# Attention and expert router: a later reciprocal of the gates, and a reordered set-up

## The chip, the cores and the metric

The kernel runs on one core of a Trainium2 chip. The metric is device time in microseconds (us) of one execution, from launch to end. The time before is the median of three runs; the profile is that of one more execution, with its own time. Engines are called as in the profile: PE (TensorE; PEld is its weight load), DVE (VectorE), ACT (ScalarE), POOL (GpSimd) and SP (SyncE, which here only issues DMAs).

## The reference

Two stages in one launch. First block-sparse attention: 4 sequences of 768 tokens, 8 heads of 64, 24 blocks of 32 tokens; a query block sees its neighbours, the first and the last block, and three random blocks whose numbers come in as int64.

```python
mask = np.abs(blk_i - blk_j) <= 1
mask = mask | (blk_i == 0) | (blk_j == 0) | (blk_i == n_blocks - 1) | (blk_j == n_blocks - 1)
for qb in range(n_blocks):
    for kb in sampled_blocks[qb]:
        mask[qb*block:(qb+1)*block, kb*block:(kb+1)*block] = True
scores = np.where(mask, scores, -1e9)
...
x = attn_out.transpose(0, 2, 1, 3).reshape(B * S, H * D)
```

Then a router over 8 experts for the 3072 rows x of 512: logits are the cosines of x with the expert embeddings over tau, the expert is the argmax, the gate its softmax probability, and the row's output is `gate * relu(x @ w1[e]) @ w2[e]`.

## The kernel before

**Attention** takes about the first half of the span. The 4 sequences have 4 pairs of heads each; a pair is 12 units (2 halves of the queries times 6 chunks of keys), so a sequence is 48 units, and `u % 48` is the unit that a plan speaks of. For each unit the program writes down `attend_fast(u)` and then `score_fast(u + 2)` (the loop in `attention_fast`, L835 to L861):

- `score_fast`: PE adds the mask (`sc<-qmask,kmask`, bf16) and the scores (`sc<-qt,kt`, f32) in PSUM; ACT takes the exponential `e` (L342).
- `attend_fast`: DVE adds the `e` of a half up in `esum` (L355 for the first two, L357 for the others), PE multiplies `e` with the values into `av` (L360). Behind the sixth unit ACT copies one half of `av` to `part` (L364), and DVE adds the other to it as `at` (L366). There is one `av` buffer: the next half's first `av` matmul on PE has to wait for `at`.
- `turn_fast`: every sixth unit PE transposes half of the next pair's keys and queries into the PSUM tile `turn` (L322); `kt` (L325) and `qt` (L326) are its copies in SBUF.
- `settle`, at the fourth unit of the next half: PE transposes `at` back (`back`, L388), sums `esum` (L395); DVE divides (L398 to L408) and writes the rows `x` and the partial logits `part`. `squares` then lets POOL square `x` and add it up in a tree (L419, L423). `turn`, `back`, `tp` (the turned embeddings) and `rk` (of `rank`) share one PSUM buffer, `small`.

**Routing** of a finished sequence is a generator, `route`, that is taken a step further at certain units of the next sequence; `after_sequence` holds the table of these units, written by hand. Its steps: sums on POOL (norm, partial logits); norm, logits and maximum on DVE; exponential on ACT and choice on DVE (`pick`, `oh`); counts `seen` (six additions, L514) and the gate's denominator on POOL (`ex_l`, `x` column 512; L516 to L519), one by one between the squares of the same unit; the reciprocal of the gates on DVE (L521); then the DMAs of the rows `x` to DRAM. `rank` multiplies `oh` and `seen` on PE (`rk`, L535 to L537). All steps are put down with `issue_after` behind the last `esum` and `e`, and a scheduler then merges them into each engine's in-order queue.

**Experts** follow: 27 tiles of 128 rows, whose weights (4 MB a tile) come by DMA into three buffers.

**Set-up** before unit 0: `load_first` loads the first pair in halves and the block numbers (`ids`), POOL makes the identity, `build_mask` makes `kmask` and `qmask` (DVE, POOL, a matmul `qr` on PE, and a copy of one half each by DVE and ACT, L148), `turn_fast(0, 0)` turns the first half. At u = 3 `build_experts` normalises the expert embeddings: squares on ACT (L194), power on POOL (L195), three DVE steps (L196 to L198), four transposes on PE (`tp`, L201), copies on DVE (`en`, `back`).

Of the kernel before, what the change touches and what calls it, by code (L numbers as in the profile page):

```python
# [11 lines left out]
F32 = mybir.dt.float32  # L12
I32 = mybir.dt.int32
# [34 lines left out]
def two_banks(k, name):  # L48
    return k.small.tile([P, 2, 512], F32, name=name, tag="small")
# [9 lines left out]
def build_ident(k):  # L59
    k.ident = k.const.tile([P, P], F32, name="ident")  # L60
    make_identity(k.nc, k.ident[:])
# [29 lines left out]


def load_ids(k):
    nc, pool = k.nc, k.setup
    k.ids = pool.tile([NB, NRAND], I32, name="ids")
    words = dataclasses.replace(k.blocks.tensor, shape=[NB, 2 * NRAND], dtype=I32)
    with nc.allow_non_contiguous_dma(reason="low words of the block numbers"):
        nc.sync.dma_start(out=k.ids, in_=bass.AP(tensor=words, offset=0, ap=[[2 * NRAND, NB], [2, NRAND]]))


def block_mask(k, exact=False):

    nc, pool = k.nc, k.setup
    dif = iota(k, "dif", [NB, NB], [[1, NB]], mult=-1)
    col = iota(k, "col", [NB, NB], [[1, NB]])
    row = iota(k, "row", [NB, NB], [[0, NB]], mult=1)
    m = pool.tile([NB, NB], F32, name="m")
    nc.vector.tensor_tensor(out=m, in0=dif, in1=dif, op=ALU.mult)
    nc.vector.tensor_scalar(out=m, in0=m, scalar1=1.5, scalar2=None, op0=ALU.is_le)
    for val in (0.0, float(NB - 1)):  # L110
        for pos in (col, row):
            ins = nc.vector.scalar_tensor_tensor(out=m, in0=pos, scalar=val, in1=m, op0=ALU.is_equal, op1=ALU.max)
    ids_f = pool.tile([NB, NRAND], F32, name="ids_f")
    with k.tc.issue_after(ins.ins):
        nc.vector.tensor_copy(out=ids_f, in_=k.ids)
    for r in range(NRAND):
        nc.vector.scalar_tensor_tensor(out=m, in0=col, scalar=ids_f[:, r:r + 1], in1=m,
                                       op0=ALU.is_equal, op1=ALU.max)
    both = pool.tile([NB, 2, D], F32 if exact else BF16, name="both")
    if not exact:  # L120
        nc.gpsimd.memset(both, 0.0)
    nc.vector.tensor_scalar(out=both[:, :, 0:NB], in0=m.unsqueeze(1).broadcast_to([NB, 2, NB]), scalar1=1.0,
                            scalar2=-NEG, op0=ALU.subtract, op1=ALU.mult)
    return both
# [62 lines left out]


def build_experts(k):
    nc, pool = k.nc, k.setup  # L190
    emb, tau = k.emb_rows, k.tau_rows
    sq = pool.tile([E, DM], F32, name="emb_sq")
    nrm = pool.tile([E, 1], F32, name="emb_nrm")
    nc.scalar.activation(sq, emb, ACT.Square, accum_out=nrm)  # L194
    nc.gpsimd.tensor_tensor(out=nrm, in0=nrm, in1=k.half[0:E, 0:1], op=ALU.pow)  # L195
    nc.vector.tensor_scalar(out=nrm, in0=nrm, scalar1=1e-6, scalar2=tau[:, 0:1], op0=ALU.add, op1=ALU.mult)  # L196
    nc.vector.reciprocal(out=nrm, in_=nrm)
    nc.vector.tensor_scalar(out=emb, in0=emb, scalar1=nrm[:, 0:1], scalar2=None, op0=ALU.mult)  # L198
    tp = two_banks(k, "tp")[:, 0]
    for c in range(ND):  # L200
        nc.tensor.transpose(tp[:, c * E:(c + 1) * E], emb[:, c * P:(c + 1) * P], k.ident[0:E, 0:E])  # L201
    k.en = k.const.tile([P, ND, E], F32, name="en")
    nc.vector.tensor_copy(out=k.en, in_=tp[:, 0:ND * E].rearrange("p (c e) -> p c e", e=E))
    k.back = k.const.tile([P, NPAIR, D + E], F32, name="back")
    for h in range(2):
        rows = slice(D * h, D * (h + 1))
        nc.vector.tensor_copy(out=k.back[rows, :, 0:D],
                              in_=k.ident[rows, rows].unsqueeze(1).broadcast_to([D, NPAIR, D]))
        nc.vector.tensor_copy(out=k.back[rows, :, D:D + E], in_=k.en[rows])


def load_pair(k, g, parts=(0, 1, 2), engine=None):
# [96 lines left out]
def turn_fast(k, g, part):  # L309

    nc = k.nc
    if part == 0:
        k.turned[g] = [k.tp.tile([P, NC, 2, D], F32, name=f"{n}t", tag=f"{n}t") for n in ("k", "q")]
    ps = two_banks(k, "turn")[:, :, 0:2 * NQ * D].rearrange("p r (n c t) -> p r n c t", n=2, t=D)
    chunks = slice(part * NQ, (part + 1) * NQ)
    for n in range(2):
        src = k.loaded[g][n][part] if g == 0 else k.loaded[g][n][:, :, chunks]
        for c in range(NQ):
            for r in range(2):
                toks = slice(D * r, D * (r + 1))  # L320
                for h in range(2):
                    nc.tensor.matmul(ps[D * h:D * (h + 1), r, n, c, :], lhsT=src[toks, h, c, :],  # L322
                                     rhs=k.ident[toks, toks], start=True, stop=True)
    kt, qt = [t[:, chunks].rearrange("p c r t -> p r c t") for t in k.turned[g]]
    nc.vector.tensor_copy(out=kt, in_=ps[:, :, 0])  # L325
    nc.scalar.mul(out=qt, in_=ps[:, :, 1], mul=SCALE)  # L326


# [142 lines left out]
def route(k, b):  # L471
# [47 lines left out]
    nc.gpsimd.tensor_scalar(out=gate, in0=gate, scalar1=1e-9, scalar2=None, op0=ALU.add)  # L519
    yield  # L520
    nc.vector.reciprocal(out=gate, in_=gate)  # L521
    drams = (k.x_early, k.x_dram) if b < EARLY else (k.x_dram,)
    for dram in drams:
        for c in range(NC):
# [266 lines left out]
def after_sequence(n, b):  # L791

    routing = partial(next, route(n, b), None)
    plan = [(7, routing), (10, routing), (11, routing), (12, routing), (14, partial(rank, n, b))]
    plan += [(13, routing)] + [(15 + NC * (i // 4), routing) for i in range(NC * (1 + (b < EARLY)))]
    if b == EARLY - 1:
        step = partial(next, dispatch_early(n), None)
        plan += [(u, step) for u in range(16, 39) if u % 3]
        plan += [(40, partial(fetch_rows, n, 0)), (41, partial(fetch_rows, n, 1))]
        step = partial(next, fetch_weights(n, 0, 4), None)  # L800
        plan += [(u, step) for u in (27, 27, 33, 33, 39, 39, 45, 45)]
    if b == EARLY:
        step = partial(next, fetch_weights(n, 1, 4), None)
        plan += [(u, step) for u in (3, 3, 9, 9, 27, 27, 33, 33)]
        plan += [(44, partial(prepare, n, 0))]
    return plan


def attention_fast(n, ctx):
    def pool(name, bufs, **kw):  # L810
        return ctx.enter_context(n.tc.tile_pool(name=name, bufs=bufs, **kw))

    n.acc, n.big = pool("acc", 1, space=PSUM), pool("big_f", 2, space=PSUM)
    n.ld, n.tp, n.ep = pool("ld", 3), pool("tp", 2), pool("ep", 4)
    pairs = B * NPAIR
    units, per = pairs * 2 * NC, 2 * NC
    n.masked = []
    setup = ExitStack()
    n.setup = setup.enter_context(n.tc.tile_pool(name="setup", bufs=1))
    load_first(n)  # L820
    build_ident(n)
    build_mask(n)
    turn_fast(n, 0, 0)
    score_fast(n, 0)
    score_fast(n, 1)
    turn_fast(n, 0, 1)
    with n.tc.issue_after(n.masked[0]), n.tc.issue_after(n.masked[1]):
        build_consts(n)
    load_pair(n, 1)
    load_experts(n)  # L830
    zero = n.const.tile([1, XW], F32, name="zero")
    n.nc.vector.memset(zero, 0.0)
    n.nc.sync.dma_start(n.x_dram[N:N + 1, :], zero)
    plan = []
    for u in range(units):  # L835
        g = u // per
        if u % per == 0 and g + 2 < pairs:
            load_pair(n, g + 2)
        if u % NC == 3 and NC < u < units - 2 * NC:
            settle(n, u // NC - 1)  # L840
        if u % NC == 4 and NC < u < units - 2 * NC:
            squares(n, u // NC - 1)
        if u == 3:
            with n.tc.issue_after(n.summed.ins), n.tc.issue_after(n.exps.ins):
                build_experts(n)
            setup.close()
        if u % (per * NPAIR) == 0 and u:
            plan = after_sequence(n, u // (per * NPAIR) - 1)
        for when, what in plan:
            if when == u % (per * NPAIR):  # L850
                with n.tc.issue_after(n.summed.ins), n.tc.issue_after(n.exps.ins), n.tc.issue_after(n.tick.ins):
                    what()
        attend_fast(n, u)
        if u + 2 < units:
            score_fast(n, u + 2)
        if u % NC == NC - 1 and g + 1 < pairs:
            turn_fast(n, g + 1, u % per // NC)
        if u in (units - NC - 1, units - 2):
            settle(n, u // NC - 1)
        if u >= units - 4 and u % 2 == 0:  # L860
            squares(n, 2 * B * NPAIR - 3 + (u == units - 2))  # L861
# [175 lines left out]
```

## Time and profile before

| what | value |
|---|---|
| median of 3 runs | 791.93 us (791.09 to 792.12) |
| the profiled execution's own time | 791.82 us |
| its span, first to last instruction | 790.1 us |
| PE busy | 752.5 us (95%) |
| DVE, ACT, POOL busy | 324.6, 200.4, 214.6 us |
| mean granted clock of PE | 0.980 |
| attention, experts | 0 to about 383 us, from there to the end |

The profiled execution lies 1.72 us above its span and 0.11 us below the median. How to read it: a busy PE does not say that PE is at its best, since its clock has two levels (granted clock 1.00 is 2.4 GHz, 0.50 is 1.2 GHz). An idle stretch in front of an instruction is put down to what released it. The order of instructions on an engine is fixed when the program is built.

### The profile page before, as it was taken

How to read it: one execution, taken by the hardware profiler on the slowest of the kernel's cores; microseconds unless marked ns; L12 is line 12 of the kernel's file. 1: busy time of each engine (PE TensorE's matmuls, PEld its weight loads, DVE VectorE, ACT ScalarE, POOL GpSimd, SP SyncE). 2: the span in 40 equal slices, each digit the busy share in tenths (PEclk: the TensorE clock that was granted, in tenths of full speed). 3: DMA queues.
4: the chain of work that ended last, by engine and by line, in shares of the span. 5: the costliest groups of instructions: out<-in, count | busy, mean ns of one | idle time of the engine just before them, and what ended most of it. 6: DMA issues, size and time to landing. Idle time of an engine off the chain costs nothing.

```text
span 790.1 us, 22711 instructions
## 1 busy us (share of the span) xinstructions
PE 752.5 (95%) x10020; PEld 493.2 (62%) x10020; DVE 324.6 (41%) x629; ACT 200.4 (25%) x297; POOL 214.6 (27%) x388
## 2 busy tenths in 40 slices
PE   6999997999979998899999999999999999999993
PEld 3555554555545555455768768677677687786771
DVE  5566664666658766566581111111111111111110
ACT  3454553555534554345200000000000000000000
POOL 2233362443443466242512112111121121110110
PEclk9999998999999999899999999999999999999997
DMA  5012112531144563321599989989989999899890
GB/s 181 25 44 60 63 62 75 145 103 38 52 127 137 189 221 120 119 69 57 191 317 400 354 332 319 336 300 332 337 306 339 337 308 337 320 326 330 301 334 32
DMA packets 69221, 165.49 MB, mean 209 GB/s; under 512 B 3756, under 2 KB 16556, under 8 KB 69110
## 3 DMA queue, kind: packets, MB, share of 16 engines
q1 hardware_dynamic: 64086, 149.60, 54.5%
q0 software_dynamic: 4480, 13.91, 4.5%
q8 instruction: 82, 1.34, 0.7%
q10 hardware_dynamic: 544, 0.39, 0.1%
q14 instruction: 29, 0.24, 0.1%
HBM read 148.14 MB, written 16.54 MB: 208 GB/s over the span
## 4 chain that ended last, share of the span: by engine, by line
PE 83%; issue 5%; POOL 4%; DVE 3%; DMA 2%; ACT 1%; SPq 0%; POOLq 0%; DVEq 0%; ACTq 0%
PE hp L769 22%; PE yp L782 21%; PE sc L339 18%; PE av L360 15%; PE back L395 2%; PE turn L322 2%; PE xg_ps L754 1%; PE back L388 1%; ACT e L342 1%; DMA out_dram<-y,slot_l 1%; POOL sq L423 1%; DVE esum L357 1%; DMA vld<-in_v_dram 1%; POOL nrm L483 1%; DMA ids<-in_sampled_blocks_dram 0%
## 5 line engine op out<-in xcount | busy, mean ns | idle before, releaser
L769 PEld LDWEIGHTS hp<-xgt,w 128*128 128x128 f32 x1728 | 197.1, 192 | 12.1 <-issue 11.5
L769 PE MATMUL hp<-xgt,w 128*128 128x128 f32 x1728 | 198.1, 275 | 0.0
L782 PE MATMUL yp<-w,h 128*128 128x512 f32 x432 | 189.9, 592 | 0.0
L342 ACT ACTIVATE e<-sc 128x768 f32<-128x768 f32 x192 | 155.5, 810 | 130.4 <-PE sc L339 130.0
L360 PE MATMUL av<-e,vld 64*64 64x384 f32 x1536 | 167.6, 501 | 16.5 <-DVE at L366 15.8
L339 PE MATMUL sc<-qt,kt 64*64 64x384 f32 x1536 | 165.8, 495 | 0.1
L357 DVE TENSOR_TENSOR esum<-esum,e 128x768 f32<-128x768 f32 x128 | 134.6, 1052 | 74.7 <-ACT e L342 71.8
L782 PEld LDWEIGHTS yp<-w,h 128*128 128x128 f32 x432 | 80.1, 190 | 90.3 <-issue 90.0
L772 ACT ACTIVATE h<-hp 128x512 f32<-128x512 f32 x27 | 16.1, 597 | 359.7 <-PE hp L769 359.7
L360 PEld LDWEIGHTS av<-e,vld 64*64 64x64 f32 x1536 | 51.6, 136 | 70.6 <-ACT e L342 25.4
L785 POOL DMA_INDIRECT out_dram<-y,slot_l x22 | 22.3, 1013 | 267.6 <-DVE y L784 255.5
L423 POOL TENSOR_TENSOR sq<-sq 128x192 f32<-128x192 f32 (+1 forms) x186 | 89.7, 482 | 12.5
L339 PEld LDWEIGHTS sc<-qt,kt 64*64 64x64 f32 x1536 | 61.1, 136 | 41.2 <-issue 38.0
L776 DVE TENSOR_SCALAR h<-hp 128x512 f32<-128x512 f32 x27 | 18.7, 692 | 160.1 <-PE hp L769 159.8
L784 DVE TENSOR_SCALAR y<-yp,xg 128x512 f32<-128x512 f32 x27 | 20.3, 751 | 152.8 <-PE yp L782 152.8
L419 POOL TENSOR_TENSOR sq<-x 128x384 f32<-128x384 f32 x31 | 26.4, 851 | 196.8 <-DVE part L408 137.1
L339 PE MATMUL sc<-qmask,kmask 64*64 64x384 bf16 x768 | 68.3, 330 | 0.0
L339 PEld LDWEIGHTS <-kmask 64*64 64x64 bf16 x768 | 25.5, 109 | 33.4 <-issue 33.2
L355 DVE TENSOR_TENSOR esum<-e 128x768 f32<-128x768 f32 x32 | 31.0, 968 | 17.3 <-ACT e L342 17.3
L326 ACT ACTIVATE qt<-turn 128x384 f32<-128x384 f32 x32 | 15.7, 490 | 61.6 <-DVE kt L325 59.4
L322 PEld LDWEIGHTS turn<-ident,kld 64*64 64x64 f32 x768 | 17.9, 137 | 14.9 <-issue 5.8
L714 POOL DMA_INDIRECT xg<-x_dram,slot_l x24 | 24.7, 1029 | 7.3 <-issue 7.3
(159 smaller groups left out, 394.8 us busy)
## 6 DMA issues: line engine op xcount, KB each, us to landing
w<-in_moe_w_dram SPq DMA_DIRECT2D x54, 2048.0 KB
w<-in_moe_w_dram SPq DMA_DIRECT2D x16, 512.0 KB
x_dram<-x SPq DMA_DIRECT2D x24, 256.5 KB
vld<-in_v_dram SPq DMA_DIRECT2D x16, 384.0 KB
kld<-in_k_dram SPq DMA_DIRECT2D x15, 384.0 KB
qld<-in_q_dram SPq DMA_DIRECT2D x15, 384.0 KB
x_early<-x SPq DMA_DIRECT2D x12, 256.5 KB
ticks<-dens SPq DMA_DIRECT2D x32, 0.0 KB
```

The source lines that it names most:

```text
L322: nc.tensor.matmul(ps[D * h:D * (h + 1), r, n, c, :], lhsT=src[toks, h, c, :], rhs=k.ident[toks, toks], start=True, stop=True)
L339: nc.tensor.matmul(ps[D * r:D * (r + 1), h, 0:HALF], lhsT=rows[D * h:D * (h + 1), keys], rhs=cols[D * h:D * (h + 1), queries], start=first ...
L342: k.exps = nc.scalar.activation(e, ps[:, :, 0:HALF], ACT.Exp)
L355: k.summed = nc.vector.tensor_tensor(out=k.esum, in0=k.first, in1=e, op=ALU.add)
L357: k.summed = nc.vector.tensor_tensor(out=k.esum, in0=k.esum, in1=e, op=ALU.add)
L360: nc.tensor.matmul(k.av[D * h:D * (h + 1), r, 0:HALF], lhsT=v[D * r:D * (r + 1), h, kc, :], rhs=e[D * r:D * (r + 1), h, :], start=(kc == 0 ...
L419: nc.gpsimd.tensor_tensor(out=sq, in0=x, in1=x, op=ALU.mult)
L423: nc.gpsimd.tensor_tensor(out=out, in0=sq[:, :, 0:width], in1=sq[:, :, width:2 * width], op=ALU.add)
L714: k.nc.gpsimd.indirect_dma_start(out=x[:, :], out_offset=None, in_=(k.x_dram if late else k.x_early)[:, :], in_offset=bass.IndirectOffsetO ...
L769: nc.tensor.matmul(hp[:, f, :], lhsT=w1[:, d, (f0 + f) * P:(f0 + f + 1) * P], rhs=xt[:, d, :], start=(d == 0), stop=(d == ND - 1))
L782: nc.tensor.matmul(yp, lhsT=h[:, f, :], rhs=w2[:, f, :], start=(f == 0), stop=(f == NF - 1))
L785: nc.gpsimd.indirect_dma_start(out=k.out[:, :], out_offset=bass.IndirectOffsetOnAxis(ap=slot, axis=0), in_=y[:, :], in_offset=None, bounds ...
```

## The change

Six edits:

1. `route` yields once more behind the reciprocal of the gates, and `after_sequence` calls that step at unit 17 where it was 13, and the DMAs of `x` at 21, 27 and 33 where they were 13, 15, 21 and 27. Two steps of loading the second expert tile's weights go from 27 to 15.
2. `load_ids` loads the 6 words of each of the 24 rows in one run, and `block_mask` reads the low words from the tile; before, the DMA picked 72 single words.
3. `turn_fast(0, 0)` is put down ahead of `build_mask`, and its `kt` copy runs on ACT (the first half of the first pair alone).
4. `build_experts` is a generator of three steps, taken at u = 2, 4 and 7, where the whole ran at u = 3.
5. The row of zeros behind `x_dram` is set by POOL in the first of these steps, where DVE set it before unit 0; its DMA follows it.
6. The set-up pool is closed at u = 7.

```diff
@@ load_ids, block_mask
-    k.ids = pool.tile([NB, NRAND], I32, name="ids")
+    k.ids = k.setup.tile([NB, NRAND, 2], I32, name="ids")
...
-        nc.sync.dma_start(out=k.ids, in_=bass.AP(tensor=words, offset=0, ap=[[2 * NRAND, NB], [2, NRAND]]))
+    k.nc.sync.dma_start(out=k.ids.rearrange("p r w -> p (r w)"),
+                        in_=bass.AP(tensor=words, offset=0, ap=[[2 * NRAND, NB], [1, 2 * NRAND]]))
...
-        nc.vector.tensor_copy(out=ids_f, in_=k.ids)
+        nc.vector.tensor_copy(out=ids_f, in_=k.ids[:, :, 0])
@@ build_experts
     nc.gpsimd.tensor_tensor(out=nrm, in0=nrm, in1=k.half[0:E, 0:1], op=ALU.pow)
+    zero = k.const.tile([1, XW], F32, name="zero")
+    nc.gpsimd.memset(zero, 0.0)
+    nc.sync.dma_start(k.x_dram[N:N + 1, :], zero)
+    yield
     nc.vector.tensor_scalar(out=nrm, in0=nrm, scalar1=1e-6, scalar2=tau[:, 0:1], op0=ALU.add, op1=ALU.mult)
...
     nc.vector.tensor_scalar(out=emb, in0=emb, scalar1=nrm[:, 0:1], scalar2=None, op0=ALU.mult)
+    yield
     tp = two_banks(k, "tp")[:, 0]
@@ turn_fast
-    nc.vector.tensor_copy(out=kt, in_=ps[:, :, 0])
+    (nc.vector.tensor_copy if g or part else nc.scalar.copy)(out=kt, in_=ps[:, :, 0])
@@ route
     nc.vector.reciprocal(out=gate, in_=gate)
+    yield
@@ after_sequence
-    plan += [(13, routing)] + [(15 + NC * (i // 4), routing) for i in range(NC * (1 + (b < EARLY)))]
+    plan += [(17, routing)] + [(21 + NC * (i // 4), routing) for i in range(NC * (1 + (b < EARLY)))]
...
-        plan += [(u, step) for u in (3, 3, 9, 9, 27, 27, 33, 33)]
+        plan += [(u, step) for u in (3, 3, 9, 9, 15, 15, 33, 33)]
@@ attention_fast
+    turn_fast(n, 0, 0)
     build_mask(n)
-    turn_fast(n, 0, 0)
...
-    zero = n.const.tile([1, XW], F32, name="zero")
-    n.nc.vector.memset(zero, 0.0)
-    n.nc.sync.dma_start(n.x_dram[N:N + 1, :], zero)
-    plan = []
+    plan, experts = [], build_experts(n)
...
-        if u == 3:
+        if u in (2, 4, 7):
             with n.tc.issue_after(n.summed.ins), n.tc.issue_after(n.exps.ins):
-                build_experts(n)
-            setup.close()
+                next(experts)
+            if u == 7:
+                setup.close()
```

What this does to the engines' queues, at three places. First DVE, behind the first sequence, from the choice of the experts on (`x<-x` is the reciprocal of the gates). Before:

```order
L510 TENSOR_TENSOR oh<-pick,mx 128x48
L357 TENSOR_TENSOR esum<-esum,e 128x768
L521 RECIPROCAL x<-x 128x6
L366 TENSOR_TENSOR at<-av,part 128x384
L355 TENSOR_TENSOR esum<-e 128x768
L325 COPY kt<-turn 128x2x3x64
L357 TENSOR_TENSOR esum<-esum,e 128x768
L539 COPY count<-rk 128x8
L541 TENSOR_TENSOR mine<-rk,oh 128x48
L542 TENSOR_REDUCE rank<-mine 128x6
L357 TENSOR_TENSOR esum<-esum,e 128x768 x2
L398 TENSOR_REDUCE dens<-back 128x6
```

Now (lines are six or seven further down in the changed file):

```order
L516 TENSOR_TENSOR oh<-pick,mx 128x48
L363 TENSOR_TENSOR esum<-esum,e 128x768
L372 TENSOR_TENSOR at<-av,part 128x384
L361 TENSOR_TENSOR esum<-e 128x768
L331 COPY kt<-turn 128x2x3x64
L363 TENSOR_TENSOR esum<-esum,e 128x768
L546 COPY count<-rk 128x8
L548 TENSOR_TENSOR mine<-rk,oh 128x48
L549 TENSOR_REDUCE rank<-mine 128x6
L363 TENSOR_TENSOR esum<-esum,e 128x768 x2
L404 TENSOR_REDUCE dens<-back 128x6
L527 RECIPROCAL x<-x 128x6
```

The reciprocal moved from in front of `at` to behind the first step of the next `settle`. The same move stands in the second and the third sequence's routing.

Second PE, where the embeddings are turned (`tp`). Before, between the two halves of the scores of unit 6:

```order
L339 MATMUL sc<-qmask,kmask 64x384
L339 MATMUL sc<-qt,kt 64x384 x2
L201 MATMUL tp<-ident,emb 128x8 x4
L339 MATMUL sc<-qt,kt 64x384 x2
L360 MATMUL av<-e,vld 64x384 x4
```

Now, behind the scores of unit 8, one `av` and one `sc` after the first turn of the second pair:

```order
L345 LDWEIGHTS kmask
L345 MATMUL sc<-qmask,kmask 64x384
L345 MATMUL sc<-qt,kt 64x384 x4
L206 MATMUL tp<-ident,emb 128x8 x4
L366 MATMUL av<-e,vld 64x384 x4
```

`tp` moved two units down, to a place where the PSUM buffer `small` still holds the turned keys and queries of the second pair.

Third ACT, from the start. Before:

```order
L148 ACT_TABLE_LOAD
L148 CAST qmask<-qr 128x384
L326 ACTIVATE qt<-turn 128x2x3x64
L342 ACTIVATE e<-sc 128x768 x2
L326 ACTIVATE qt<-turn 128x2x3x64
L342 ACTIVATE e<-sc 128x768 x3
L194 ACTIVATE emb_sq,emb_nrm<-emb 8x512
```

Now:

```order
L331 ACT_TABLE_LOAD
L331 COPY kt<-turn 128x2x3x64
L332 ACTIVATE qt<-turn 128x2x3x64
L147 CAST qmask<-qr 128x384
L348 ACTIVATE e<-sc 128x768 x2
L332 ACTIVATE qt<-turn 128x2x3x64
L348 ACTIVATE e<-sc 128x768 x2
L194 ACTIVATE emb_sq,emb_nrm<-emb 8x512
```

`kt` and `qt` stand ahead of the mask's copy, and the squares of the embeddings one `e` earlier.

## Rows read from the trace of the kernel before

**Rows 1.** The page's head.

```profile
span 790.1 us, 22711 instructions
```

**Rows 2.** What PE waited for: us in total, times, longest us.

```profile
PE av L360 <- DVE at L366: 15.8, 4, 5.2
...
PE tp L201 <- DVE emb L198: 2.0, 1, 2.0
```

**Rows 3.** Timeline behind the first sequence: start us, us, what [idle before <-releaser].

```profile
122.49 1.58 DVE L357 TENSOR_TENSOR esum<-esum,e 128x768 f32<-128x768 f32 x1
...
128.02 0.20 DVE L521 RECIPROCAL x<-x 128x6 f32<-128x6 f32 x1 [3.95 <-POOL x L519]
128.13 0.52 DVE L366 TENSOR_TENSOR at<-av,part 128x384 f32<-128x384 f32 x1
...
128.70 1.56 PE L360 MATMUL av<-e,vld 64*64 64x384 f32 x8 [4.90 <-DVE at L366]
```

**Rows 4.** Timeline of POOL in the same stretch.

```profile
122.42 0.83 POOL L419 TENSOR_TENSOR sq<-x 128x384 f32<-128x384 f32 x1 [3.22 <-DVE x L405]
123.22 0.91 POOL L514 TENSOR_TENSOR seen<-seen,oh 128x8 f32<-128x8 f32 x1
...
124.64 0.20 POOL L514 TENSOR_TENSOR seen<-seen,oh 128x8 f32<-128x8 f32 x1
...
126.23 0.20 POOL L514 TENSOR_TENSOR seen<-seen,oh 128x8 f32<-128x8 f32 x1
...
127.72 0.26 POOL L519 TENSOR_SCALAR x<-x 128x6 f32<-128x6 f32 x1
```

**Rows 5.** Timelines of DVE and PE behind the second and the third sequence.

```profile
217.36 1.58 DVE L357 TENSOR_TENSOR esum<-esum,e 128x768 f32<-128x768 f32 x1
...
223.56 1.56 PE L360 MATMUL av<-e,vld 64*64 64x384 f32 x8 [5.19 <-DVE at L366]
...
312.23 1.58 DVE L357 TENSOR_TENSOR esum<-esum,e 128x768 f32<-128x768 f32 x1
...
318.43 1.56 PE L360 MATMUL av<-e,vld 64*64 64x384 f32 x8 [5.20 <-DVE at L366]
```

**Rows 6.** Stretches: us, busy us of PE, PEld, DVE, ACT, POOL, PEclk, DMA, GB/s.

```profile
127.60:134.45 6.85, 5.75 (x40) 2.17 (x40) 2.92 (x5) 1.30 (x2) 0.30 (x2) 0.50 0.52 153
...
223.20:226.60 3.40, 3.04 (x24) 1.34 (x28) 1.64 (x3) 0.49 (x1) 0.00 (x0) 0.50 0.75 203
...
315.35:322.20 6.85, 3.77 (x28) 1.68 (x32) 1.96 (x4) 0.97 (x2) 2.04 (x11) 0.50 0.65 206
...
21.80:25.20 3.40, 3.40 (x32) 1.95 (x28) 0.96 (x1) 1.33 (x2) 0.00 (x0) 0.50 0.00 0
```

**Rows 7.** Timeline of the set-up, around the turned embeddings.

```profile
18.85 0.75 POOL L195 TENSOR_TENSOR emb_nrm<-emb_nrm,half 8x1 f32<-8x1 f32 x1 [14.34 <-ACT emb_sq L194]
...
20.64 0.41 PE L201 MATMUL tp<-ident,emb 8*128 8x8 f32 x4 [1.98 <-DVE emb L198]
...
22.81 0.18 PEld L360 LDWEIGHTS av<-e,vld 64*64 64x64 f32 x1 [0.44 <-ACT e L342]
```

**Rows 8.** Timeline of an undisturbed stretch, behind a turn.

```profile
37.67 0.83 PE L360 MATMUL av<-e,vld 64*64 64x384 f32 x8
...
39.12 0.82 PE L360 MATMUL av<-e,vld 64*64 64x384 f32 x8
...
39.52 0.49 ACT L326 ACTIVATE qt<-turn 128x384 f32<-128x384 f32 x1 [1.49 <-DVE kt L325]
```

**Rows 9.** Timeline of the start.

```profile
4.99 0.15 DVE L115 CAST ids_f<-ids 24x3 f32<-24x3 int32 x1 [0.66 <-DMA ids<-in_sampled_blocks_dram]
...
8.12 1.05 PE L339 MATMUL sc<-qmask,kmask 64*64 64x384 bf16 x8
...
9.30 2.62 PE L339 MATMUL sc<-qt,kt 64*64 64x384 f32 x16
```

**Rows 10.** Timeline of DVE, the first step of the next settle.

```profile
138.88 0.17 DVE L398 TENSOR_REDUCE dens<-back 128x6 f32<-128x12 f32 x1
```

More of the change, by code (lines that the diff above doesn't have):

```diff
@@ L93, in load_ids @@
 def load_ids(k):
-    nc, pool = k.nc, k.setup
-    k.ids = pool.tile([NB, NRAND], I32, name="ids")
+    k.ids = k.setup.tile([NB, NRAND, 2], I32, name="ids")
     words = dataclasses.replace(k.blocks.tensor, shape=[NB, 2 * NRAND], dtype=I32)
-    with nc.allow_non_contiguous_dma(reason="low words of the block numbers"):
-        nc.sync.dma_start(out=k.ids, in_=bass.AP(tensor=words, offset=0, ap=[[2 * NRAND, NB], [2, NRAND]]))
+    k.nc.sync.dma_start(out=k.ids.rearrange("p r w -> p (r w)"),
+                        in_=bass.AP(tensor=words, offset=0, ap=[[2 * NRAND, NB], [1, 2 * NRAND]]))
 def block_mask(k, exact=False):
@@ L521, in route @@
     nc.vector.reciprocal(out=gate, in_=gate)
+    yield
     drams = (k.x_early, k.x_dram) if b < EARLY else (k.x_dram,)
```

## Prediction

> **What bounds the kernel now.** I read the page's head first [rows 1]: the span of 790.1 us, to which everything is compared; the sum below is made against this execution's own time of 791.82 us, 0.11 us under the median of the three runs. PE sets the end nearly everywhere, so the next view is what PE itself waited for [rows 2]. Two entries matter: 15.8 us in 4 waits of `av` for `at`, and 2.0 us in one wait of the turned embeddings `tp` for DVE. The third view is the timeline around the longest of these [rows 3]. The reader is to see a queue blocked by its head: on DVE the reciprocal of the gates (L521) sat 3.95 us until POOL had ended L519; `at`, which needs nothing from POOL, stood right behind it; and PE, whose next `av` needs `at`, stood still for 4.90 us. The second and the third sequence show the same with 5.19 and 5.20 us [rows 5]. The fourth wait, the remaining 0.5 us of the 15.8, is of another kind and stays.
>
> The last view, the stretches with their granted clock [rows 6], shows what follows a stop: at 127.6, 223.2, 315.35 and 21.8 us the clock went to 0.50 (1.2 GHz), for 6.85, 3.40, 6.85 and 3.40 us. Before each of them PE had stood still, for 4.90, 5.19, 5.20 and, at the embeddings, 1.98 us [rows 3, 5, 7]. PE was busy 5.75, 3.04, 3.77 and 3.40 us in them; at full clock that work takes half, so they cost 2.88, 1.52, 1.88 and 1.70 us more. I count these with the waits.
>
> **The change part by part.**
>
> *The reciprocal at unit 17.* It removes the three waits and adds none of their size, but `at` is not free at once: the `esum` ahead of it took 1.58 us and ended at 124.07 [rows 3]. With the reciprocal gone, `at` runs from there for 0.52, and PE starts 0.05 later, as it did at 128.70: at 124.64. PE had stopped at 128.70 - 4.90 = 123.80, so 0.84 us of the wait stay. In the same way the second sequence keeps 217.36 + 1.58 + 0.57 - (223.56 - 5.19) = 1.14, the third 312.23 + 1.58 + 0.57 - (318.43 - 5.20) = 1.15 [rows 5]. So 15.29 - 3.13 = 12.16 us of waiting go, and with them the three half-clock stretches, 2.88 + 1.52 + 1.88 = 6.28 us. Together 18.44 us.
>
> What is late next there? Two things hang on POOL. `rank` on PE needs the sixth `seen`, which ended at 126.43 while DVE stood still [rows 4]. Two units of 1.45 us [rows 8] behind 124.64 PE gets there at about 127.5. In the changed kernel one `esum` of DVE falls into POOL's chain. How they get on is seen in [rows 3, 4]: the `seen` that met an `esum` took 0.91 us, the next one 0.20, and the `esum` that met L419 took 1.58. They ran one after the other. So I add 0.95 us, and the sixth `seen` ends at 127.4, just in time: nothing. The reciprocal itself now stands behind the next `settle`'s first step, which ran at 138.88 [rows 10] and moves up by the 4.06 us of wait and the 2.88 us of clock to about 131.9; POOL's L519 ended at 127.98 and, 0.95 later, at 128.9. Its 0.20 us are hidden too, as long as DVE is not late with the next `at`.
>
> The Trainium skill (SBUF — State Buffer, Who interferes with whom) says that a VectorE instruction with two SBUF inputs and a GpSimd instruction that reads SBUF exclude each other, the first one holding the port for its whole length. This trace agrees (0.91 us against 0.20), and it speaks against this edit: POOL's chain was short because DVE stood still, and by that rule it grows as soon as DVE works. My sum has one such meeting; with more of them it is the first rival.
>
> *The DMAs of `x`* (12, 12 and 6 of them) go four to six units later on SP's queue, behind the loads of the next pair; those no longer queue behind a DMA that waits for the reciprocal. The first sequences' rows are read by a gather at unit 40, 13 units after the last of them at 27. *The second expert tile's weights* (two calls) go ahead of them, to unit 15. Both nothing: nobody waits for these loads [rows 2]; if that cover went, a gather or the first tile would wait, and would be seen on PE at the start of the experts.
>
> *The embeddings in three steps.* The power on POOL (18.85, 0.75 us) and the three DVE steps no longer end in front of a waiting `tp` [rows 7]: two units lie between. The wait of 1.98 us goes, the 0.44 us by which ACT's `e` was late behind it, and the half clock, 1.70: 4.12 us. But at its new place `tp` waits for the buffer `small`, until ACT has read the `turn` in it. In an undisturbed stretch `qt` ends at 39.52 + 0.49 = 40.01, and PE would go on with `av` at 39.12 [rows 8]. So PE waits 0.89 us and a release of 0.06, which is 0.95 us of new wait; the transposes themselves were paid before as well. Net 3.17 us. Bounds: nothing, if ACT is early, to 1.98, the old wait.
>
> *The start.* DVE idled 0.66 us for the block numbers [rows 9]. The trace does not show the load in rows. It is later at most by nothing, for it has a third of the pieces, and earlier by 0.66 us at most, since the steps of the mask ahead of it on DVE end there. I take 0.66: 24 pieces behind the first load of keys instead of 72. *`kt` on ACT, turned ahead of the mask*: between the eight mask matmuls (until 9.17) and the scores at 9.30 lay 0.13 us for `qt` [rows 9]; both copies are now done before the mask. 0.13 us, from 0 to 0.13. *The zeros on POOL*: nothing, POOL idled there for 14.34 us [rows 7]; their DMA is read by the experts alone.
>
> **Sum**: 18.44 + 3.17 + 0.79 = 22.4 us. 791.82 - 22.4 = **769.4 us**. Unknown in it: the start (0 to 0.8), `tp` (1 either way), what remains in front of `at` (0.5 to 1.5 each, so 1.5 either way).
>
> **The rivals.**
>
> 1. *POOL becomes the next wait.* If a second `esum` meets the chain, the sixth `seen` ends at 128.4 and PE waits 0.9 us in front of `rank`, three times: 2.8 us, 772.2. For it: my margin is 0.1 us. Against: DVE has idle time there. This is the outcome by the skill's rule of the exclusive port, with two meetings instead of one.
> 2. *The clock still falls.* The stops that remain (0.84 to 1.15 us, and 0.95 for `tp`) are half as long as the shortest that a fall followed, 1.98 [rows 7], and I know none that it did not follow except 0.5 us [rows 2]. If it falls behind the three, at 1.52 to 1.70 us each as in the shortest stretches [rows 6], that is 4.8 us: 774.2.
> 3. *Slower than before: DVE blocks in `settle`.* At its new place the reciprocal holds up more, `dens`, `inv`, `x`, `part`, two `esum` and `at`, if POOL is still not done. To eat up 22.4 us it must wait 7.5 us each time, so L519 has to end near 139.5 instead of 128.9. Every one of the 17 POOL instructions behind L419 would have to wait for an `esum` of 0.95 us for that (16 us). Half a pair has only five `esum`. Then 792 and more.
> 4. *The reciprocal is not what holds `at`.* If `at` needed something else that ended at 128, nothing of the 18.44 goes, and the reordered set-up might lose what it wins: 788 to 792. Against it: `at` started 0.11 us behind the reciprocal, in all three places.
>
> **How the numbers follow.** A measurement of this kernel tells about 0.2% (1.6 us) from no change. My forecast gets 0.73, rival 1 0.11, rival 2 0.12, rival 3 0.02, rival 4 0.02. The first three are all faster by far more than 0.2%: 0.96. Rival 3 is the slower case, 0.02, and rival 4 stands for no change, 0.02. The forecast alone reaches from 766.5 to 772, rivals 1 and 2 to about 774.5; both can add up. The range of **766 to 775** takes in these, and leaves out some 0.15.
>
> **What would show it.** Right: on DVE no idle time in front of the reciprocal; PE's waits of `av` for `at` down from 15.8 to 3 to 4 us, the longest near 1.15; no stretch at 0.50 in the three sequences, nor behind the embeddings; `tp` waiting about 1 us for ACT's `qt`; first mask matmul 0.5 to 0.8 us earlier than 8.12; experts shifted as a block. Wrong: waits of PE in front of `rk` for POOL (rival 1); granted clock 0.50 behind waits of 1 us (rival 2); idle time of DVE between `dens` and its next step (rival 3); `av` still waiting 5 us (rival 4).

## The result and the profile after

The changed kernel takes **770.78 us** (median of 4 runs, 770.67 to 772.14), the kernel before 791.65 us (4 runs, 791.09 to 792.12): a ratio of 0.9741, 95% interval 0.9724 to 0.9757, so 20.9 us less. The forecast was 769.4 us. The profiled execution took 770.67 us. The page's head, to be read against [rows 1]:

```profile
span 769.0 us, 22707 instructions
...
PE 743.8 (97%) x10020; PEld 491.8 (64%) x10020; DVE 324.9 (42%) x627; ACT 200.6 (26%) x298; POOL 221.0 (29%) x389
...
PEclk9999999999999999999999999999999999999997
```

What PE waited for (us in total, times, longest us), the answer to [rows 2]:

```profile
PE av L366 <- DVE at L372: 3.3, 4, 1.1
PE back L401 <- issue: 1.6, 2, 1.3
PE tp L206 <- ACT qt L332: 0.7, 1, 0.7
PE sc L345 <- DVE qmask L147: 0.6, 1, 0.6
PE qr L143 <- DVE both L121: 0.5, 1, 0.5
```

The waits of `av` for `at` fell from 15.8 to 3.3 us, the wait of `tp` from 2.0 to 0.7. The second line is new: PE stood still inside `back`, and nothing that the profile shows released it. The timeline behind the first sequence, the answer to [rows 3, 4] (start us, us, what, [idle before]):

```profile
117.88 1.58 DVE L363 TENSOR_TENSOR esum<-esum,e 128x768 f32<-128x768 f32 x1
119.39 0.54 DVE L372 TENSOR_TENSOR at<-av,part 128x384 f32<-128x384 f32 x1
...
124.51 0.91 POOL L525 TENSOR_SCALAR x<-x 128x6 f32<-128x6 f32 x1
...
127.42 0.18 DVE L527 RECIPROCAL x<-x 128x6 f32<-128x6 f32 x1
...
119.98 0.88 PE L366 MATMUL av<-e,vld 64*64 64x384 f32 x8 [0.80 <-DVE at L372]
...
123.05 0.42 PE L542 MATMUL rk<-oh,before 128*128 128x48 f32 x2
```

`at` now runs right behind the `esum` of 1.58 us, and PE waits 0.80 us. The reciprocal has no idle time in front of it: POOL had been done for 2.00 us (124.51 + 0.91 to 127.42). `rk` has no wait either. The four stretches behind these places, the answer to [rows 6]:

```profile
119.98:126.83 6.85, 6.85 (x146) 4.26 (x150) 4.05 (x8) 2.84 (x4) 5.12 (x16) 1.00 0.45 143
208.46:211.86 3.40, 3.40 (x43) 1.71 (x44) 2.12 (x3) 1.36 (x3) 3.32 (x12) 1.00 0.75 247
299.18:306.03 6.85, 6.85 (x146) 4.26 (x150) 4.05 (x8) 2.84 (x4) 5.11 (x16) 1.00 0.70 263
23.56:26.96 3.40, 3.40 (x52) 1.95 (x56) 1.91 (x5) 1.46 (x2) 0.00 (x0) 1.00 0.02 5
```

All four are at full clock; before, all four were at 0.50.

**Where the 21 us came from.** The starts of PE's mask matmuls in the timeline mark the units; a period of six units without anything special lasts 10.73 us.

| stretch | before | after | gain | forecast |
|---|---|---|---|---|
| start to the first mask matmul | 8.12 | 7.57 | 0.55 | 0.66 |
| from there to unit 12 | 26.59 | 22.46 | 4.13 | 3.30 |
| the six units with routing, first sequence | 19.36 | 12.45 | 6.91 | |
| the same, second | 18.31 | 12.71 | 5.60 | |
| the same, third | 18.67 | 12.62 | 6.05 | 18.44 for the three |
| the six with the stop of 0.28 us | 10.73 | 11.20 | -0.47 | 0 |
| the six with the stop of 1.31 us | 11.22 | 12.70 | -1.48 | 0 |

The first matmul of the experts moved from 382.98 to 361.92 us, by 21.06, and the experts behind it by the same amount. The new loss, seen closer: PE, then what SP issued ahead of it.

```profile
258.42 0.35 PE L401 MATMUL back<-ones,esum 64*64 64x1 f32 x15
260.08 0.65 PE L401 MATMUL back<-ones,esum 64*64 64x1 f32 x33 [1.31 <-issue]
```

```profile
249.92 1.80 SPq L532 DMA_DIRECT2D x_dram<-x  x4
251.92 1.10 SPq L743 DMA_DIRECT2D w<-in_moe_w_dram  x2
253.12 0.44 SPq L224 DMA_DIRECT2D vld<-in_v_dram  x1
...
254.16 1.11 SPq L224 DMA_DIRECT2D qld<-in_q_dram  x1
```

The DMA view has a queue q8, which brings instructions in 82 pieces of 16 KB. From 249.4 to 257.5 us no piece of it ran, and the next came from 257.6 to 258.6 among other data (queue: packets, MB, share of 16 engines; first the whole span, then the view of 249.4 to 257.5 us, then that of 257.5 to 258.7):

```profile
q8 instruction: 82, 1.34, 0.7%
...
q1 hardware_dynamic: 737, 1.65, 86.2%
q14 instruction: 1, 0.01, 0.4%
...
q1 hardware_dynamic: 147, 0.45, 95.2%
q8 instruction: 1, 0.02, 5.3%
```

PE ran on 1.46 us after that piece had landed. That q8 is PE's queue is shown by a count further down. The Trainium skill (Runtime: NRT & Kernel Launch, Terms) says that an engine's instructions lie in a small memory of its own that is refilled in blocks of 16 KiB; the pieces of this trace have that size.

### The profile page after: what moved, and what is told of

Read it like the earlier page. It is cut to its first block, busy times and chain, and to the rows that moved or that the text cites. A ratio compares the mean times of both kernels' runs of the same rounds, so it can differ in the third digit from the quotient of the medians.

```text
span 769.0 us, 22707 instructions
## 1 busy us (share of the span) xinstructions
PE 743.8 (97%) x10020; PEld 491.8 (64%) x10020; DVE 324.9 (42%) x627; ACT 200.6 (26%) x298; POOL 221.0 (29%) x389
## 4 chain that ended last, share of the span: by engine, by line
PE 83%; issue 6%; DVE 5%; POOL 4%; ACT 1%; DMA 1%; POOLq 0%; DVEq 0%; ACTq 0%
PE hp L776 22%; PE yp L789 21%; PE sc L345 17%; PE av L366 14%; PE back L401 2%; PE turn L328 2%; DVE esum L363 2%; PE xg_ps L761 1%; PE back L394 1%; DMA out_dram<-y,slot_l 1%; ACT e L348 1%; POOL nrm L489 1%; POOL sq L429 1%; POOL part L499 1%; DVE x L411 0%
## 5 line engine op out<-in xcount | busy, mean ns | idle before, releaser
L366 PE MATMUL av<-e,vld 64*64 64x384 f32 x1536 | 161.8, 490 | 4.1 <-DVE at L372 3.3
L345 PE MATMUL sc<-qt,kt 64*64 64x384 f32 x1536 | 160.2, 486 | 0.0
L792 POOL DMA_INDIRECT out_dram<-y,slot_l x22 | 22.4, 1016 | 267.4 <-DVE y L791 255.3
L345 PE MATMUL sc<-qmask,kmask 64*64 64x384 bf16 x768 | 66.6, 325 | 0.6 <-DVE qmask L147 0.6
L345 PEld LDWEIGHTS <-kmask 64*64 64x64 bf16 x768 | 25.1, 107 | 33.3 <-issue 32.8
L401 PE MATMUL back<-ones,esum 64*64 64x1 f32 x1536 | 26.8, 191 | 1.6 <-issue 1.6
## 6 DMA issues: line engine op xcount, KB each, us to landing
x_dram<-x SPq DMA_DIRECT2D x24, 256.5 KB
x_early<-x SPq DMA_DIRECT2D x12, 256.5 KB
```

The lines of the kernel that those rows point to most:

```text
L345: nc.tensor.matmul(ps[D * r:D * (r + 1), h, 0:HALF], lhsT=rows[D * h:D * (h + 1), keys], rhs=cols[D * h:D * (h + 1), queries], start=first ...
L366: nc.tensor.matmul(k.av[D * h:D * (h + 1), r, 0:HALF], lhsT=v[D * r:D * (r + 1), h, kc, :], rhs=e[D * r:D * (r + 1), h, :], start=(kc == 0 ...
L401: nc.tensor.matmul(sums[D * s:D * (s + 1), t, h, r:r + 1], lhsT=esum[D * r:D * (r + 1), h, cols], rhs=k.ones[D * r:D * (r + 1), 0:1], star ...
L792: nc.gpsimd.indirect_dma_start(out=k.out[:, :], out_offset=bass.IndirectOffsetOnAxis(ap=slot, axis=0), in_=y[:, :], in_offset=None, bounds ...
```

## The experiments

The runs went to several chips, on which the kernel before took 791.3 to 793.4 us; versions are compared by their ratio to it.

**The change in three parts.** e_recip is the kernel before with edit 1, e_emb with edits 4 to 6, e_start with edits 2 and 3.

```diff
-    plan += [(13, routing)] + [(15 + NC * (i // 4), routing) for i in range(NC * (1 + (b < EARLY)))]
+    plan += [(17, routing)] + [(21 + NC * (i // 4), routing) for i in range(NC * (1 + (b < EARLY)))]
```

> The kernel before with nothing but the reciprocal of the gates at unit 17, the copies of x at 21, 27 and 33, and the second tile's weights at 15. My theory (the reciprocal in front of `at` held PE three times, and the clock fell behind it): the three periods of six units come down from 19.36, 18.31 and 18.67 us to about 12.6 each (18.5 us), and PE stops some 1.6 to 2 us in `back` for late instructions, so about 775 us. The embeddings keep their wait of 2.0 us and their half clock. Rival, that `at` waits for something else: no gain, 790 to 792 us.

> The kernel before with nothing but the embeddings in three steps and the zeros on POOL. My theory: the 2.0 us wait of `tp` for DVE becomes one of 0.7 to 0.95 us for ACT's `qt`, the clock doesn't fall behind it, and the mask matmul of unit 12, at 34.7 us before, comes about 3.9 us earlier: 787.5 to 788.5 us. Rival, that the start gave a part of what unit 12 won in the changed kernel: 789 us or more.

> The kernel before with nothing but the block numbers in rows, the first turn ahead of the mask and its `kt` on ACT. My theory: the first mask matmul comes at about 7.6 us and not at 8.1, nothing else changes, 791.0 to 791.4 us, which is no difference that can be told from the run to run spread. Rival, that the start decides when the clock first rises: more than 1 us faster or slower.

| part | ratio to before | 95% | us |
|---|---|---|---|
| e_recip | 0.9794 | 0.9768 to 0.9820 | -16.3 |
| e_emb | 0.9966 | 0.9952 to 0.9980 | -2.7 |
| e_start | 0.9993 | 0.9983 to 1.0002 | none that can be told |

(us by 1 less the ratio, times 793.36.) The parts add up to the whole within their intervals. In e_recip the three periods are 12.44, 12.71 and 12.62 us, as forecast, and the stops in `back` are there without any of the other edits; the old wait of `tp` is there too, and the clock behind it (PE's waits, then the stretch of 21.6 to 25.1 us):

```profile
PE av L360 <- DVE at L366: 3.3, 4, 1.1
PE back L395 <- issue: 2.1, 2, 1.4
PE tp L201 <- DVE emb L198: 2.0, 1, 2.0
```

```profile
21.60:25.10 3.50, 3.50 (x33) 1.89 (x25) 1.13 (x2) 0.87 (x2) 0.00 (x0) 0.51 0.03 5
```

So edit 1 makes both the large gain and the new loss. In e_emb `tp` waits 0.66 us for `qt`, and unit 12 comes 3.3 us earlier (34.71 to 31.39), not 3.9. e_start missed its forecast: its first mask matmul comes at 8.46 us, not at 7.6, since PE had its first keys at 4.95 us (4.06 in the changed kernel) and DVE the block numbers at 5.32 (4.38). The ten profiles of kernels with the whole new set-up have 7.54 to 7.57 us (three) or 8.01 to 8.04 (seven), those with the old start 8.07 (e_emb), 8.12 (before) and 8.49 (e_recip). So the 0.55 us in the table above are the better of two outcomes.

That the start can't be told has one more reason: PE's first matmuls run at half pace, and the moment at which that ends differs from execution to execution. The same eight `av` matmuls of unit 0, in e_start and in the changed kernel:

```profile
12.89 1.54 PE L359 MATMUL av<-e,vld 64*64 64x384 f32 x8
```

```profile
11.74 0.84 PE L366 MATMUL av<-e,vld 64*64 64x384 f32 x8
```

**A reciprocal that waits elsewhere.** e_r14 puts it at unit 14, on DVE behind `at` and the first `esum`, ahead of `kt`.

```diff
-    plan += [(17, routing)] + [(21 + NC * (i // 4), routing) ...
+    plan += [(14, routing)] + [(21 + NC * (i // 4), routing) ...
```

> The changed kernel with the reciprocal at unit 14: on DVE it then stands behind `at` and the first `esum`, ahead of `kt`. My theory (any instruction of DVE that waits for POOL's L525 holds up all that is behind it): the reciprocal waits some 3 us (120.9 to about 124.1 in the first sequence), `kt` and `qt` come that much later, and PE waits for `qt` in front of `rk` about 2.3 us, three times: 6.9 us, so about 777.7; if the clock falls behind a stop of this length, 1.5 to 1.7 us more each, about 782.5. Rival, that only a reciprocal ahead of `at` costs anything: 770.8.

It took 788.35 us, a ratio of 0.9946 (0.9928 to 0.9965): most of the gain is lost. The timeline behind the first sequence, then the stretches behind the three stops (the granted clock is the number behind POOL's count):

```profile
124.06 0.26 POOL L525 TENSOR_SCALAR x<-x 128x6 f32<-128x6 f32 x1
124.36 0.19 DVE L527 RECIPROCAL x<-x 128x6 f32<-128x6 f32 x1 [3.24 <-POOL x L525]
124.47 0.52 DVE L331 COPY kt<-turn 128x384 f32<-128x384 f32 x1
...
125.04 0.88 PE L345 MATMUL sc<-qt,kt 64*64 64x384 f32 x8 [2.33 <-DVE kt L331]
```

```profile
127.00:130.40 3.40, 3.40 (x64) 2.18 (x60) 1.47 (x6) 0.81 (x1) 0.00 (x0) 0.50 0.02 5
219.20:229.40 10.20, 10.20 (x130) 6.22 (x130) 4.94 (x15) 2.48 (x4) 2.05 (x4) 0.50 0.01 3
...
319.00:325.00 6.00, 6.00 (x134) 3.70 (x135) 4.03 (x10) 2.77 (x5) 0.00 (x0) 1.00 0.03 7
```

The theory held in its mechanism and its size (3.24 us on DVE, 2.33 us on PE), not in the place: PE stops at `sc` for `kt`, ahead of `rk`. The rival falls. It also gave something not asked for: three stops of the same length (2.33, 2.32, 2.34 us) were followed by 3.4 us, 10.2 us and no time at half clock, so the three periods cost 16.67, 20.15 and 15.18 us where the changed kernel has 12.45, 12.71 and 12.62.

**Do the stops in `back` come from late instructions?** Five kernels. after_again is the changed kernel as it is.

> The changed kernel once more, with no edit, beside the other three. If PE's stops in `back` belong to the program, they are again at the same two places (0.3 and 1.3 us); if they depend on the chip or on the execution, they are elsewhere or of another length. The three periods with routing must again be 12.4 to 12.7 us, and the ratio to the kernel before 0.972 to 0.976.

Its ratio is 0.9739 (0.9723 to 0.9756) and its stops are 0.57 and 1.30 us, at the same two places: the places belong to the program. The length of the first does not: e_burst and e_wlate below have the same program up to there, and those six units took 11.22 and 10.95 us in them, 11.48 here and 11.20 in the changed kernel's first profile. e_spread takes the copies of `x` apart, e_burst puts more weights into the burst:

```diff
@@ e_spread
-    [(21 + NC * (i // 4), routing) for i in range(...)]
+    [(18 + i, routing) for i in range(...)]
@@ e_burst
-    (27, 27, 33, 33, 39, 39, 45, 45)
+    (27, 27, 33, 33, 33, 33, 45, 45)
```

> The changed kernel with the copies of x one to a unit, from unit 18 on, and not four at once at 21, 27 and 33. My theory (PE's stops of 1.31 and 0.28 us in `back`, put down to `issue`, are its instructions coming late behind bursts of data): the piece of instructions no longer comes 9.6 us behind the one before, both stops go, and the time falls by 1.6 to 2.0 us to about 768.9. Rival, that the stops come from something else in the program, as from the code of the dispatch steps there: they stay and the time stays within 0.4 us of the changed kernel's 770.8.

> The changed kernel with two more pieces of the first tile's weights (512 KB each) at unit 33, from unit 39: six DMAs of weights and x become eight in the burst ahead of the 1.31 us stop. My theory (PE's instructions come late behind data): the piece of instructions in the burst comes later than 9.6 us behind the one before, and PE's stop there grows from 1.3 to 2 us or more: 771.5 to 773, by the changed kernel's 770.8. Rival, that the data have nothing to do with it: the stop stays at 1.3 us or moves without growing, the time within 0.5 us of the changed kernel's.

e_spread: 0.9719 (0.9703 to 0.9736), which can't be told from after_again. The stop of the first sequence is gone (10.74 us for those six units), and that of 1.3 us fell to 0.37 and 0.18, but further on PE waited 0.24 for ACT and 0.82 for `at`; nothing was won. e_burst: 0.9755 (0.9739 to 0.9771), the stop 1.43 us and the piece at 257.85 us, as late as before: the growth did not come. By 257.5 us the DMAs had moved 1.65 MB in the changed kernel, of the 3.2 MB that SP had asked for by then (four copies of 256.5 KB, two pieces of 512, three loads of 384), so what I added had probably not begun to move when the piece came; this kernel could not tell. Next, no weights at all in that stretch: e_quiet with `x` spread as well, e_wlate with `x` left in fours.

```diff
-        plan += [(u, step) for u in (27, 27, 33, 33, 39, 39, 45, 45)]
+        plan += [(u, step) for u in (41, 41, 43, 43, 45, 45, 47, 47)]
```

> The changed kernel with the copies of x one to a unit from 18 on, and with the first tile's weights (eight pieces of 512 KB) at units 41 to 47 and not 27 to 45, so that no weights are loaded where PE stopped 1.3 us in `back` and where it stopped behind ACT after that. My theory (PE's instructions come late behind the data of other queues): those three periods of six units, 11.3, 12.7 and 10.8 to 12.5 us in the changed kernel, come to 11.3, 11.2 and 10.8, and the time is 1.5 to 3 us less, 769.6 to 771 where the changed kernel took 772.6. Rival, that the stops belong to the program at this place (its many small instructions) whatever is loaded: a stop of over 1 us stays there.

> The changed kernel with nothing but the first tile's weights at units 41 to 47 and not 27 to 45; the copies of x stay four at once at 21, 27 and 33. It tells which data the late instructions wait behind. If the weights and the copies of x add up: the stop of 0.3 to 0.6 us of the first sequence stays (no weights there), and the one of 1.3 us in the second falls to 0.3 to 0.6 too; the time is 1 to 2.5 us under the changed kernel's (ratio to before 0.9715). If the copies of x alone make it: 1.3 us again and no gain (0.974).

e_quiet: 769.04 us, 0.9718 (0.9702 to 0.9734), by its interval not to be told from the changed kernel; the periods tell more. The three are 11.30, 11.22 and 10.76 us, those of the kernel before; what is left is one stop of 0.54 us, later. The rival falls. e_wlate: 0.9727 (0.9712 to 0.9742). The stop of 1.3 us is gone from its place, and two stand where the weights went (PE's rows, then SP's issue ahead of the second):

```profile
270.71 0.45 PE L401 MATMUL back<-ones,esum 64*64 64x1 f32 x17 [0.84 <-issue]
282.93 0.16 PE L401 MATMUL back<-ones,esum 64*64 64x1 f32 x1 [1.09 <-issue]
...
272.07 2.47 SPq L743 DMA_DIRECT2D w<-in_moe_w_dram  x4
```

So the stops move with the weights, and neither theirs nor the copies' place alone decides. In all twelve stops of over 0.5 us in `back` or `turn`, in eight kernels, PE ran on 1.27 to 1.58 us after a piece of q8 had landed. A count shows that PE waits for its instructions there: each of the twelve came after exactly 449 + 256 n instructions of PE in the trace (matmuls, weight loads and its sequencer's), where n is the number of pieces that had landed before the late one. For the stop of 1.31 us these are 10,945 and 41; elsewhere 7,105 and 26, or 11,969 and 45. So a piece carries 256 instructions of PE, and PE stopped where it had used up the last of them. (Two stops of 1.0 us in front of an `av`, in e_emb and e_start, are put down to "issue" too, but lie 3.2 to 3.3 us behind a piece, after 11,090 instructions with 42 pieces landed, so PE had over 100 left; their cause is open.) Why a piece is late, the trace doesn't show, since it doesn't have the moment at which it was asked for; that it stands behind data is inferred from the stops that move with the data.

**What is left in front of `at`.** e_late puts the routing behind the first half pair:

```diff
-    plan = [(7, routing), (10, routing), (11, routing), (12, routing), (14, partial(rank, n, b))]
-    plan += [(17, routing)] + [(21 + NC * (i // 4), routing) ...
+    plan = [(7, routing), (14, routing), (15, routing), (16, routing), (19, partial(rank, n, b))]
+    plan += [(22, routing)] + [(23 + i, routing) ...
```

> The changed kernel with the whole chain of the routing behind the first half pair: its second to fourth steps at units 14, 15 and 16 and not 10, 11 and 12, `rank` at 19, the reciprocal at 22, the copies of x one to a unit from 23, the early dispatch from 20. My theory of what is left of the three waits of `av` (0.80, 1.06 and 0.98 us): DVE stood 1.25 us waiting for POOL's power in the second step, so the `esum` ahead of `at` starts late. With the steps behind `at` the three waits fall to 0.3 us or less, as in a sequence without routing, and the periods from 12.4 to 12.7 to about 11.9 (10.73 and the `rank`): 2 to 2.8 us less than the changed kernel, 768 to 769. Rival, that `at` waits for the `esum` of 1.58 us alone, which collides with POOL's squares: the three waits stay over 0.6 us.

0.9722 (0.9705 to 0.9738), no gain that can be told. The three waits of 0.80, 1.06 and 0.98 us are gone, as the theory had it, and the rival falls, but others took their place, in front of `rk` and, with the early dispatch, at other `at`:

```profile
PE av L366 <- DVE at L372: 2.9, 4, 1.1
PE rk L542 <- ACT qt L332: 2.4, 3, 0.9
```

Two versions then kept every step off the places ahead of `at`, `tp` and `rk` two units behind a turn (unit 8, unit 20), and the last one the weights and `x` apart:

```diff
@@ best
+    plan = [(7, routing), (14, routing), (15, routing), (15, routing), (20, partial(rank, n, b))]
+    plan += [(20, routing)] + [(21 + i, routing) ...
+        plan += [(u, step) for u in range(20, 40) if 1 < u % 6 < 5 for _ in range(1 + (u % 6 == 2 or u == 39))]
+        if u in (2, 4, 8):
@@ best2, against best
+    ... [(21 + 2 * i, routing) ...
+        plan += [(u, step) for u in range(20, 41) if 1 < u % 6 < 5 for _ in range(1 + (u % 6 == 2))]
+        plan += [(u, step) for u in (28, 30, 32, 34, 40, 42, 44, 46)]
```

> The changed kernel with the routing's second to fourth steps at units 14, 15 and 15, `rank` and the reciprocal at 20, x one to a unit from 21, the early dispatch at the third to fifth units of each six from 20, and `tp` at unit 8. My theory: a step that lands on DVE behind `at` and not ahead of it costs PE nothing, and a tile in the small PSUM buffer costs nothing two units behind the turn. So the waits for `at` (3.3 us), for `qt` in front of `tp` (0.8) and in front of `rk` (2.4 in the run before) go to under 1 us together, and the stops in `back` (1.9) as with x spread: 772.6 less 4 to 6.5 us, 766 to 768.5. Rival, that the work only moves its collision: as in the run before, about 771, with waits of over 2 us somewhere else in the three sequences.

> The version before it with its three remaining stops taken up: the first tile's weights one piece to every second unit from 28 to 46 (36 and 38 left free), x one to every second unit from 21, and the last step of the early dispatch (its `slot_ps` waited 0.76 us for the buffer of `back`) at unit 40. My theory (late instructions where more than about 1 MB of data is asked for at once; steps behind `at` cost nothing): no stop of over 0.5 us in `back` or `turn`, no half clock before the end, waits of PE in the attention under 2 us in all behind unit 2. By the e_quiet run (769.0, its three waits of `at` 2.3 and `tp` 0.7) that is about 766, a ratio to the kernel before of 0.968. Rival, that PE's late instructions come whatever the spacing: 769 to 771 again, with a stop of over 1 us.

best: 771.07 us, 0.9735 (0.9719 to 0.9751), a miss for a reason of its own. All waits for `at`, `tp` and `rk` were gone, but late instructions stopped PE for 1.70 us in `back`, and this time the clock fell behind it (two stretches):

```profile
245.00:246.80 1.80, 0.10 (x5) 0.01 (x4) 1.47 (x3) 0.48 (x1) 0.00 (x0) 1.00 0.80 198
247.30:250.80 3.50, 3.50 (x39) 2.42 (x37) 1.20 (x5) 0.12 (x1) 1.60 (x3) 0.51 0.38 116
```

best2: **766.97 us** (765.84 to 767.86) beside 791.98 for the kernel before, 0.9684 (0.9671 to 0.9697): faster than both kernels, and as forecast. It changes the spacing of `x`, that of the weights and one step of the dispatch together, so which of them ended the stop of 1.70 us is not shown, and no run measures the 1 MB of its forecast. What PE waits for in it:

```profile
PE qr L143 <- DVE both L121: 0.9, 1, 0.9
PE sc L345 <- DVE qmask L147: 0.6, 1, 0.6
PE av L366 <- ACT e L348: 0.5, 2, 0.3
PE slot_ps L631 <- DVE part L414: 0.3, 1, 0.3
PE back L401 <- issue: 0.2, 1, 0.2
```

## Why the prediction was right, and where not

Forecast 22.4 us of gain, measured 21.15 in the profiled execution (791.82 to 770.67). The small error is in part luck: 0.84 us more gain than forecast at the listed places (0.12 and 0.72) stand against 1.95 us of loss that was not forecast at all.

- **The reciprocal: right.** 18.44 us forecast, 18.56 in the three periods. The waits that stay were forecast as 0.84, 1.14 and 1.15 us and measured 0.80, 1.06 and 0.98. e_r14 shows that the cause is the wait for L525 at the head of DVE's queue, wherever it stands there, which ends rival 4.
- **What these remaining waits are.** I put them down to the `esum` of 1.58 us. One step further back, DVE idled 1.25 us in front of the second step of the routing (`nrm`), waiting for POOL's power, and so started that `esum` late. e_late agrees, but moves the other steps of the routing too. The third sequence of e_quiet and of e_wlate shows it more closely, though no edit aimed at it: the power took 1.36 us there where it had taken 2.15 in the changed kernel, DVE did not wait, and the wait of `av` was gone. (DVE's wait in the changed kernel's first sequence; then the power in the third, in the changed kernel and in e_quiet, each with an `esum` that ran beside it.)

```profile
114.62 0.17 DVE L502 TENSOR_SCALAR nrm<-nrm 128x6 f32<-128x6 f32 x1 [1.25 <-POOL nrm L489]
...
291.44 0.96 DVE L363 TENSOR_TENSOR esum<-esum,e 128x768 f32<-128x768 f32 x1
291.48 2.15 POOL L489 TENSOR_TENSOR nrm<-nrm,half 128x6 f32<-128x6 f32 x1
```

```profile
288.85 1.36 POOL L489 TENSOR_TENSOR nrm<-nrm,half 128x6 f32<-128x6 f32 x1
288.97 2.02 DVE L363 TENSOR_TENSOR esum<-esum,e 128x768 f32<-128x768 f32 x2 [1.26 <-ACT e L348]
```

  The rule that the prediction weighed (the Trainium skill, SBUF — State Buffer, Who interferes with whom) agrees with these rows: both ran beside an `esum`, and the one that started 0.04 us behind it took 0.79 us longer than the one that started 0.12 us ahead of it. It was right that the two engines exclude each other here; the place where that costs PE time is `nrm`, not `rk`.

- **Rival 1 (POOL in front of `rk`): did not come.** In the first sequence's chain one more `seen` than before took 0.92 us and not 0.20 (0.72 more, where I had 0.95), and the sixth ended at 122.55 us, ahead of `rk` at 123.05: a margin of 0.5 us where I had 0.1. The other two sequences have the same margin.
- **Rival 2 (the clock still falls): did not come**, but it was nearer than the 0.12 I gave it. No stop of up to 1.43 us was followed by half clock in any profile, that of 1.70 us in best was. And two of e_burst's four executions, not profiled, took 774.15 and 774.47 us at a mean clock of 0.989 and 0.990, where the profiled one took 772.56 at 0.994: the clock may have fallen in them.
- **Rival 3 (DVE blocks in `settle`): did not come**; POOL was done 2.00 us ahead of the reciprocal. (Its condition was put too high: from 128.9 to 139.5 us are 10.6, so 11 meetings of 0.95 us would do, not all 17.)
- **The embeddings and the start: a gain of 4.68 us, not 3.96.** The new wait of `tp` for `qt` was of the kind forecast, 0.67 us where I had 0.95. The rest, 0.55 us, are two delays of 0.24 and 0.31 us that the lump of embedding work had caused in units 3 and 9, and that I had not counted. Of the 0.79 us at the start 0.69 came in this profile (8.12 to 7.57 us, and 0.14 in the first two units), but that is luck: most profiles with the new start have their first mask matmul at 8.01 to 8.04, and e_start's 10 executions show no gain. The way from there to unit 12 varies too, by when PE leaves half pace: 22.1 to 23.2 us in eight profiles with these edits, where the table has 22.46.
- **The step that failed: the DMAs of `x` and the weights at "nothing: nobody waits for these loads".** Nobody waits for these loads, but PE's instructions are moved by the DMA engines too, and came too late twice: the two periods with the stops lost 1.95 us. e_recip has the loss with edit 1 alone; in e_quiet, with `x` and the weights elsewhere, both periods are back at 10.74 and 11.22 us. That the pieces were late because of these loads is inferred, as said above. The copies moved by six to twelve units, too, and not by four to six.

## What to carry to other kernels

An instruction that waits for another engine holds up its whole queue; move it behind what somebody else waits for, and check at its new place that its input has long been ready. Loads that nobody waits for may not be free: here PE ran out of instructions behind a burst of 3.2 MB asked for within 5 us. Spread such loads, one or two small DMAs at a time, and look again: with `x` alone spread the longest stop was under 0.2 us in e_late, 0.37 in e_spread and 1.70 in best; with the weights spread too it was 0.16 in best2. After a long stop is gone, look at what holds up the instructions ahead of the same one: here it was again a wait for POOL, one step earlier.

## What the runs showed of the hardware

- **Late instructions.** PE stopped for 0.5 to 1.9 us with the releaser "issue" where its queue of 16 KB pieces had a gap of 7.3 to 9.8 us between two starts, and ran on 1.27 to 1.58 us after the late piece had landed. The gap alone does not tell: the changed kernel has ten of over 7.5 us between 30 and 383 us, one of them (104.3 to 112.6 us) with next to no data moved, and only the two with stops left PE without instructions. What tells is the count: PE stopped after 449 + 256 n of its instructions, n pieces having landed.
- **The clock's fall is not decided by the length of the stop alone.** Stops of 4.9 to 5.2 us were always followed by half clock, those of 2.3 us in two of three cases, those of 1.97 and 1.98 us at the embeddings in two of three (not in e_start), one of 1.93 us and one of 1.70 us were, none of up to 1.43 us was. Behind these stops the time at half clock was 3.4, 6.8 or 10.2 us.
- **PE's first matmuls run at half pace** until about 10.7 to 14.4 us of the span, by the lengths of their rows, differently in each profile. An estimate from that: the 3.7 us between the two, at half pace, are up to 1.9 us of the time.
